# Transposing q and k of a token in one full-height product, in three parts instead of two

## The chip, the core and the metric

The kernel runs on one core of a Trainium2 chip. A core has five engines that each work through their own list of instructions in order and wait for each other by semaphores: TensorE (PE in the profile; PEld is its loading of the stationary operand), VectorE (DVE), ScalarE (ACT), GpSimd (POOL) and SyncE (SP). Here POOL issues nearly all loads and SP issues small transfers and the stores. TensorE reads operands from the on-chip memory SBUF and writes to PSUM; VectorE and ScalarE copy from there. The metric is the device time of one execution, in microseconds (us): a median of 444.62 over 7 runs (444.22 to 445.11).

## The reference

Two layers in a row: causal attention with a decay bias, and a spectral mixing layer on its output.

```python
# q, k, v: (8, 8, 576, 64), s: (8, 8, 576)
scores = scale * np.matmul(q, k.transpose(0, 1, 3, 2))
cum = np.cumsum(np.maximum(s, 0.0), axis=-1)
bias = -(cum[:, :, :, None] - cum[:, :, None, :])
scores = np.where(causal, -1000000000.0, scores + np.minimum(bias, 0.0))
attn = np.exp(scores - max);  attn = attn / (sum + 1e-09)
x = np.matmul(attn, v)                       # heads put side by side: (8, 576, 512)

X = np.fft.rfft(x, axis=1)                   # the lowest 64 modes are mixed:
Yr = Xr @ w_r[m] - Xi @ w_i[m]               # w_r, w_i: (64, 512, 512), one matrix for each mode
Yi = Xr @ w_i[m] + Xi @ w_r[m]
u = x + np.fft.irfft(Y, n=576, axis=1)
out = u + np.maximum(u @ w_ch, 0.0)
```

The mode weights are 2 x 64 x 512 x 512 float32 numbers, 134 MB, and are read once. They are most of what the kernel reads from device memory.

## The kernel before

**Steps.** The 64 pairs of batch and head are worked off two heads at a time: step n of 32 has batch b = n % 8 and the heads 2g and 2g + 1 of group g = n // 8 (N = 32, NG = 4). The main loop (L564 to L590) writes for each step, in this order: POOL's loads for later steps (`load`, L568), a row of decay sums by SP (`cum_rows`, L569), scores of the first head (`scores(n, 0)`), the weighted sum of v for the second head of the step before (`av(n - 1, 1)`), mode products if due (`mode_products`), the first half of the transposes for the next step (`transposes(n + 1, 0)`), scores of the second head, the second half of the transposes, the forward Fourier product of the step before (`fft(n - 1)`), `av(n, 0)`. The order is written out by hand, and each engine keeps to it: no scheduler moves anything.

**Transposes.** q and k come as one tile of 128 partitions: 64 for q, 64 for k, each (head, group of 18 tokens) on a partition, 18 tokens of 64 numbers in a row. One load brings two steps (`loads_qk`, two buffers). `scores` needs them with the 64 numbers of a token on partitions, in `qt` and `kt` (two buffers each). So each token slot r of 18 is transposed by TensorE into PSUM (`tr_ps`, pool `tr_psum`, one buffer), and copied from there. The 18 slots go in two halves of nine. In a half, every slot takes two products of 64 rows and 64 columns: q's rows give partitions 0 to 63 of `tr_ps`, k's rows partitions 64 to 127. Then q's part is copied to `qt` by VectorE, and k's to `kt` by VectorE in the first half and by ScalarE in the second (L341 to L347). As `tr_ps` has one buffer, a half waits until both copies of the half before are done. The copy of k by ScalarE starts after the copy of q from the same tile.

**What stands around them.** `scores` (L366) makes two tiles of 128 x 896 for a head, one for even and one for odd keys, and ScalarE takes the exponential of each in two pieces (L390); in the second head `scores4` adds a small one (L361). Mode products (`modes(g, c)`, L455) multiply the transformed x of group g by the weights of chunk c: 8 modes, four weight tiles, 16 products; 8 chunks make a group. Chunks of group g run during the steps of later groups at fixed places (`mode_steps`); those of the last group run after the loop (L833 to L868). In steps 26 to 31 the loop also prepares parts of the last product with `w_ch` (`first_transposed`, L529, and `first_product`, L540): transposes of x into `xt_ps`, a copy by VectorE (L538), a product (L546).

**Loads.** POOL holds one list of loads in program order, q, k and v mixed with weights (`load`, L230). A weight tile lies in a ring of 11 or 6 buffers (`wpool`, `wpool2`), so its load waits until the products of the tile that lay there are done; a load of q and k waits for the transposes of the steps that used its buffer.

**The tail.** After the loop come the products with `w_ch` that are left (`x_transposed`, L629, with products L635, and `x_times_wch`, L648), the last group's chunks 0 to 7, the inverse transform (`gather` L688, `add_y`, `add_last`) and the sums and stores.

Of the kernel before, what the change touches and what calls it, by code (L numbers as in the profile page):

```python
# [11 lines left out]
BF16 = mybir.dt.bfloat16  # L12
# [6 lines left out]
def kernel(  # L19
# [11 lines left out]
    nc = tc.nc  # L31
    B, H, S, D = q.shape
    NM = moe_w_r.shape[0]
    DM = H * D
    P = 128
# [15 lines left out]
    NF = NT - 1  # L51
    RP = P // 4
    R = S // RP
    RH = R // 2
    W = 2 * P
    NWN = S // W
    NK = 2 * NWN
# [1 line left out]
    HP = P // 2  # L59
# [81 lines left out]
    ident16 = ap_.tile([P, P], BF16, name="ident16")  # L141
# [4 lines left out]
    loaded = {}  # L146

    def loads_qk(n):

        if n >= N:  # L150
            return []
        g, b = divmod(n, B)
        hs = slice(2 * g, 2 * g + 2)
        t = loaded[n] = loaded[n + 1] = qkpool.tile([P, 2, R * D], BF16, name="qk2", tag="qk2")
        return [
            (
                t[HP * i : HP * i + HP, x0:x1],
                src[b + x0 : b + x1, hs].rearrange("b h (p r) d -> (h p) b (r d)", r=R),
            )
            for x0, x1 in ([(0, 2)] if n else [(0, 1), (1, 2)])  # L160
            for i, src in enumerate((q, k))
        ]

    def loads_v(n):

        if n >= N:
            return []
        g, b = divmod(n, B)
        return [
            (  # L170
                v2[n % NV][:, : 2 * NWN * W].rearrange("p (w h c) -> p w h c", w=NWN, h=2)[:, :, h, P:],
                v[b, 2 * g + h, : NF * P, :].rearrange("(w p r) d -> p w (r d)", p=P, r=2),
            )
            for h in range(2)
        ]
# [27 lines left out]
    def ring_of(k):  # L203
        if k < NE:
            return None
        return int(k < LW2 and (k - NE) % (WA + WB) >= WA)
# [23 lines left out]
    def load(*lists):  # L230

        todo = [((i + 0.5) / len(l), x) for l in lists for i, x in enumerate(l)]
        for _, (dst, src) in sorted(todo, key=lambda t: t[0]):
            nc.gpsimd.dma_start(out=dst, in_=src)  # L234
# [10 lines left out]
    for n in range(N):  # L245
# [3 lines left out]
        while nt < min(w, len(wq)):  # L249
            i = ring_of(nt)  # L250
# [36 lines left out]
    with tc.tile_pool(name="cum_psum", bufs=1, space=PSUM) as cpsum:  # L287
# [5 lines left out]
            out=cum, data0=spos, data1=zer, initial=0.0, op0=ALU.add, op1=ALU.add  # L293
# [16 lines left out]
        for x in range(2):  # L310
            rows = slice(NL * x, NL * x + NL)
            nc.vector.tensor_copy(
                out=cumt4[rows, :], in_=cumt_sb[rows, NK, x::2]
# [10 lines left out]
    def cum_rows(n):  # L324
        if n >= N:
            return
        g, b = divmod(n, B)
        p0 = b * H + 2 * g
        for h in range(2):
            nc.sync.dma_start(out=qt[n % NQ][D : D + 1, h, :], in_=ncum_sb[p0 + h : p0 + h + 1, :])  # L330

    def transposes(n, half):
        if n >= N:
            return
        src = loaded[n][:, n % 2, :].rearrange("p (r d) -> p r d", d=D)[:, half * RH : half * RH + RH]
        ps = trpool.tile([P, RH, 2 * RP], BF16, name="tr_ps", tag="tr")
        for r in range(RH):
            for i in range(2):
                rows = slice(HP * i, HP * i + HP)
                nc.tensor.transpose(ps[rows, r, :], src[rows, r, :], ident16[rows, rows])  # L340
        for i, dst in enumerate((qt, kt)):  # L341
            copy = (nc.vector.tensor_copy, nc.scalar.copy)[half * i]
            to = dst[n % NQ][:D].rearrange("d h (p r) -> d h p r", r=R)
            copy(  # L344
                out=to[:, :, :, half * RH : half * RH + RH],
                in_=ps[HP * i : HP * i + HP].rearrange("d r (h p) -> d h p r", h=2),
            )  # L347

    def scores4(n, ps):
# [45 lines left out]
    def first_token(b, T):  # L395

        if b % 2 == 0:
            return T * P
        return T * P + NL if T < NF else 0

    def av(n, h):
        if n < 0:
            return
        g, b = divmod(n, B)
        pt = p_sb[(2 * n + h) % NP_]
        ps = avpool.tile([P, NT, VW], FP32, name="av_ps", tag="av")
        todo = []
        for I in range(NT):
            t0 = first_token(b, I)
            for x in range(2 * min((t0 + P - 1) // W + 1, NWN)):  # L410
                w, r = divmod(x, 2)
                o = poff[x] + t0 - w * W
                todo.append((I, r, pt[:, o : o + P], v2[n % NV][:, bass.ds((2 * w + h) * W + P - 1 + NCH * r, NCH)]))
        rows = slice(NL * h, NL * h + NL)
        todo.append((NT - 1 - b % 2, 1, p4[n % 2][rows, :], v4[g % 2][rows, b, :NCH]))

        for i, (I, r, lhsT, rhs) in enumerate(todo):
            nc.tensor.matmul(  # L418
                ps[:, I, r : r + NCH], lhsT, rhs, start=(i == 0), stop=(i == len(todo) - 1),
                skip_group_check=True,  # L420
            )
        den = rpool.tile([P, NT], FP32, name="den", tag="den")
        nc.vector.tensor_reduce(  # L423
            out=den, in_=ps[:, :, 0 : VW : NCH], axis=mybir.AxisListType.X, op=ALU.add
        )
        rcp = rpool.tile([P, NT], FP32, name="rcp", tag="rcp")
        nc.vector.reciprocal(out=rcp, in_=den)
        nc.vector.tensor_tensor(  # L428
            out=x_all[:, g, b, :, D * h : D * h + D],
            in0=ps[:, :, 1 : NCH],  # L430
            in1=rcp.unsqueeze(2).to_broadcast([P, NT, D]),
            op=ALU.mult,
        )

    def fft(n):
        if n < 0:
            return
        g, b = divmod(n, B)
        ps = auxpool.tile([P, 2, 3 * HM], FP32, name="ft_ps", tag="aux")
        for T in range(NT):  # L440
            nT = tails[T]
            for q_ in range(2):
                nc.tensor.matmul(  # L443
                    ps[HP * q_ : HP * q_ + HP].rearrange("p h f -> p (h f)"),
                    x_all[:nT, g, b, T, q_::2], Ff_sb[:nT, T, :],
                    start=(T == 0), stop=(T == NT - 1),
                    tile_position=(0, HP * q_), skip_group_check=True,
                )
        for h in range(2):
            for q_ in range(2):  # L450
                a = ps[HP * q_ : HP * q_ + HP, h, : 2 * HM].rearrange("p (r m) -> p r m", r=2)
                a = bass.AP(tensor=a.tensor, offset=a.offset, ap=[a.ap[0], [HM, 2]] + list(a.ap[1:]))
                nc.vector.tensor_copy(out=xs[g % 2][HP * h : HP * h + HP, q_, :, h, :, b, :], in_=a)  # L453
# [98 lines left out]
    def mode_products(n):  # L552
        for c in mode_steps.get(n, []):
            modes(c // NCK, c % NCK)

    with tc.tile_pool(name="sc_psum", bufs=2, space=PSUM) as scpool, \
            tc.tile_pool(name="tr_psum", bufs=1, space=PSUM) as trpool, \
            tc.tile_pool(name="av_psum", bufs=1, space=PSUM) as avpool:
        cum_rows(0)
        transposes(0, 0)  # L560
        transposes(0, 1)
        load(loads_qk(2) + loads_v(2))
        pad_p()
        for n in range(N):  # L564
            if n in (0, 2):
                nc.vector.memset(xs_flat[n // 2].bitcast(FP32), 0.0)
            tails_due = loads_tails(n // B + 1)[n % B - 3 : n % B - 2] if 2 < n % B < 5 else []
            load((loads_qk(n + LA) if n % 2 else []) + loads_v(n + LA) + tails_due, loads_w(on_chip[n]))  # L568
            cum_rows(n + 1)  # L569
            scores(n, 0)  # L570
            av(n - 1, 1)
            if n % B:
                mode_products(n)
            transposes(n + 1, 0)
            scores(n, 1)
            i = first_pairs[n - N + len(first_pairs)] if n >= N - len(first_pairs) else None
            if i is not None:
                first_transposed(i, 0)
            transposes(n + 1, 1)
            fft(n - 1)  # L580
            av(n, 0)
            if i is not None:
                first_product(i, 0)
                first_transposed(i, 1)
            if n % B == 0:
                mode_products(n)
            if i is not None:
                first_product(i, 1)
            if n == N // 2:
                nc.gpsimd.dma_start(out=wch_sb, in_=moe_w_ch.rearrange("(dt p) e -> p dt e", p=P))  # L590
        av(N - 1, 1)
        fft(N - 1)
# [278 lines left out]
    for x in range(2):  # L871
        dts = slice(x * DT // 2, (x + 1) * DT // 2)
        ps = auxpool.tile([P, DT // 2, P], FP16, name="yt_ps", tag="aux")
# [49 lines left out]
    for step in (  # L923
# [8 lines left out]
        i = int(step[1:].rstrip("ab"))  # L932
# [34 lines left out]
```

The softmax here doesn't subtract the row's maximum and nothing guards it: scores larger than these inputs give would overflow.

## Time and profile before

The profiled execution took 445.11 us, the slowest of the seven; its span, from the first to the last instruction, is 443.0 us. It has 10783 instructions.

| engine | busy, us | share of the span |
|---|---|---|
| TensorE, products | 341.2 | 77% |
| TensorE, loading | 207.2 | 47% |
| VectorE | 253.1 | 57% |
| ScalarE | 226.4 | 51% |
| GpSimd | 246.1 | 56% |

| group of instructions | count | busy, us | mean, ns |
|---|---|---|---|
| transposes of q and k, TensorE L340 | 1152 | 35.3 | 206 |
| copy to qt, VectorE L344 | 64 | 47.8 | 748 |
| copy to kt, VectorE L344 | 32 | 24.4 | 763 |
| copy to kt, ScalarE L344 | 32 | 22.9 | 714 |
| exponentials, ScalarE L390 | 256 | 141.8 | 636 |
| mode products, TensorE L463 | 480 | 43.7 | 420 |

How to read it: products overlap on TensorE, so that the mean of one is longer than its share of the busy time. The first transposes start at 10.9 us and the last at 318.9; the first mode product starts at 80.3, and the last group's chunks run from 336.5 to 409.2. Slices are 40 equal parts of the span, 11.1 us each. The row PEclk gives the clock that TensorE was granted, in tenths of the full one. A line of the timeline has start, duration, engine, source line, operation, output and inputs, how many were merged, and in brackets the idle time of the engine just before and what ended it. A line of a group has count, then busy time and mean, then idle time before and what ended it.

### The profile page before, as it was taken

The page shows a single profiled execution, that of the slowest core. Times are in us where ns is not written, and L with a number is a line of the kernel's source. Part 1 is how long each engine was busy: PE and PEld are TensorE (multiplying, and loading weights), DVE is VectorE, ACT ScalarE, POOL GpSimd, SP SyncE. Part 2 cuts the span into 40 slices and gives each one's busy share as a digit, 9 for nine tenths or more (in the row PEclk, how much of TensorE's full clock was granted, in tenths as well). Part 3 has the DMA queues.
Part 4 walks back from the last instruction along what each step waited for, and adds up shares of the span by engine and source line. Part 5 has one row for each costly group of instructions (what it writes and reads, how often), then busy time and mean ns, then how long its engine had stood idle before and what let it go on. Part 6 is the DMA issues. An engine that isn't in the chain of part 4 may idle for free.

```text
span 443.0 us, 10783 instructions
## 1 busy us (share of the span) xinstructions
PE 341.2 (77%) x4364; PEld 207.2 (47%) x4411; DVE 253.1 (57%) x574; ACT 226.4 (51%) x421; POOL 246.1 (56%) x385
## 2 busy tenths in 40 slices
PE   1787888997685996694946828888887997759994
PEld 0465665565353653362624415555554445423441
DVE  7677775676554664462634605767655454432696
ACT  1477885476544743472634504765650544220794
POOL 7766566555565656465656546465644444430495
PEclk9999998999978897887786958999997999977998
DMA  9999999999999999999999999999999999997398
GB/s 180 202 206 206 204 207 205 206 207 207 208 200 207 205 209 204 208 207 208 204 206 206 209 207 191 209 206 205 197 209 210 210 209 210 210 217 144 145 388 344
DMA packets 72768, 93.25 MB, mean 210 GB/s; under 512 B 29760, under 2 KB 31296, under 8 KB 72720
## 3 DMA queue, kind: packets, MB, share of 16 engines
q0 software_dynamic: 63408, 81.29, 104.6%
q1 hardware_dynamic: 9312, 11.29, 7.6%
q8 instruction: 34, 0.56, 0.5%
q14 instruction: 14, 0.11, 0.1%
HBM read 163.51 MB, written 9.44 MB: 390 GB/s over the span
## 4 chain that ended last, share of the span: by engine, by line
DMA 69%; PE 15%; DVE 6%; POOL 5%; issue 4%; ACT 1%; POOLq 0%; DVEq 0%
DMA w_sb<-in_moe_w_i_dram 37%; DMA w_sb<-in_moe_w_r_dram 16%; DMA qk<-in_k_dram 8%; DMA qk<-in_q_dram 4%; PE yp L463 3%; DMA x_all<-in_moe_w_r_dram 2%; PE sc_ps L382 2%; DMA y_acc<-in_moe_w_r_dram 2%; POOL w_sb L234 1%; PE sc_ps L376 1%; PE tr_ps L340 1%; DVE xs L453 1%; DVE qt L344 1%; POOL v L234 1%; PE av_ps L418 1%
## 5 line engine op out<-in xcount | busy, mean ns | idle before, releaser
L390 ACT ACTIVATE p_sb<-sc_ps,cumt_sb 128x576 f16<-128x576 f32 (+1 forms) x256 | 141.8, 636 | 33.2 <-PE sc_ps L382 32.8
L234 POOL DMA_DIRECT2D w_sb<-in_moe_w_r_dram x120 | 71.2, 595 | 59.6 <-DMA w_sb<-in_moe_w_r_dram 18.9
L234 POOL DMA_DIRECT2D w_sb<-in_moe_w_i_dram x120 | 71.0, 593 | 54.3 <-DMA w_sb<-in_moe_w_i_dram 17.7
L344 DVE COPY qt<-tr_ps 64x576 bf16<-64x576 bf16 x64 | 47.8, 748 | 59.5 <-PE tr_ps L340 59.4
L234 POOL DMA_DIRECT2D v<-in_v_dram x72 | 52.0, 722 | 39.0 <-DMA w_sb<-in_moe_w_r_dram 9.5
L382 PE MATMUL sc_ps<-qt,kt 128*128 128x320 bf16 (+2 forms) x337 | 66.7, 303 | 6.6 <-ACT kt L344 1.9
L340 PE MATMUL tr_ps<-ident,qk 64*64 64x64 bf16 x1152 | 35.3, 206 | 41.3 <-DMA qk<-in_k_dram 18.2
L463 PE MATMUL yp<-w_sb,xs 128*32 128x512 bf16 (+1 forms) x480 | 43.7, 420 | 21.4 <-DMA w_sb<-in_moe_w_i_dram 14.2
L361 ACT ACTIVATE p<-sc_ps,cumt 128x64 f16<-128x64 f32 x32 | 10.1, 314 | 89.5 <-PE sc_ps L357 89.5
L376 PE MATMUL sc_ps<-negm,ident 128*128 128x256 bf16 x256 | 54.1, 296 | 0.0
L340 PEld LDWEIGHTS <-qk 64*64 64x64 bf16 x1152 | 26.9, 119 | 57.6 <-DMA qk<-in_k_dram 19.1
L382 PEld LDWEIGHTS <-kt 128*128 128x128 bf16 x384 | 39.1, 106 | 30.8 <-ACT kt L344 8.1
L418 PE MATMUL av_ps<-v,p_sb 128*128 128x65 f16 x1024 | 43.0, 195 | 1.9 <-DVE x_all L428 0.9
L418 PEld LDWEIGHTS <-p_sb 128*128 128x128 f16 x1024 | 36.4, 98 | 9.4 <-DVE x_all L428 4.9
L453 DVE CAST xs<-ft_ps 64x128 bf16<-64x128 f32 x128 | 36.7, 286 | 3.1 <-PE ft_ps L443 1.7
L463 PEld LDWEIGHTS <-xs 128*32 128x32 bf16 (+1 forms) x512 | 19.2, 144 | 39.5 <-DMA w_sb<-in_moe_w_i_dram 15.2
L423 DVE TENSOR_REDUCE den<-av_ps 128x5 f32<-128x10 f32 x64 | 10.8, 169 | 39.7 <-PE av_ps L418 38.7
L428 DVE TENSOR_TENSOR x_all<-av_ps,rcp 128x320 f16<-128x320 f32 x64 | 31.5, 492 | 2.2
L344 ACT COPY kt<-tr_ps 64x576 bf16<-64x576 bf16 x32 | 22.9, 714 | 15.5 <-DVE qt L344 14.8
L648 PE MATMUL z_ps<-wch_sb,xs 128*128 128x512 f16 x96 | 26.1, 420 | 0.2 <-DVE xs L639 0.2
L443 PE MATMUL ft_ps<-Ff_sb,x_all 128*64 128x192 f16 (+1 forms) x320 | 24.5, 267 | 1.0 <-DVE x_all L428 1.0
L344 DVE COPY kt<-tr_ps 64x576 bf16<-64x576 bf16 x32 | 24.4, 763 | 0.4
(113 smaller groups left out, 423.6 us busy)
## 6 DMA issues: line engine op xcount, KB each, us to landing
w_sb<-in_moe_w_r_dram POOLq DMA_DIRECT2D x120, 256.0 KB, 8.4
w_sb<-in_moe_w_i_dram POOLq DMA_DIRECT2D x117, 256.0 KB, 9.0
out_dram<-r_w SPq DMA_DIRECT2D x16, 512.0 KB, 2.8
v<-in_v_dram POOLq DMA_DIRECT2D x72, 64.0 KB, 7.4
qk<-in_q_dram POOLq DMA_DIRECT2D x15, 288.0 KB, 8.0
qk<-in_k_dram POOLq DMA_DIRECT2D x15, 288.0 KB, 9.2
x_all<-in_moe_w_i_dram POOLq DMA_DIRECT2D x6, 256.0 KB, 7.7
y_acc<-in_moe_w_r_dram POOLq DMA_DIRECT2D x4, 256.0 KB, 7.2
```

The lines of the kernel that those rows point to most:

```text
L234: nc.gpsimd.dma_start(out=dst, in_=src)
L340: nc.tensor.transpose(ps[rows, r, :], src[rows, r, :], ident16[rows, rows])
L344: copy(out=to[:, :, :, half * RH : half * RH + RH], in_=ps[HP * i : HP * i + HP].rearrange("d r (h p) -> d h p r", h=2),)
L376: nc.tensor.matmul(ps[:, bass.ds(w * S, W)], ident16, negm[:, bass.ts(r, W)], start=True, stop=False, skip_group_check=True,)
L382: nc.tensor.matmul(ps[:, c0 : c0 + i1 - i0], keys[:, w, r, :], qh[:, i0:i1], start=False, stop=True, skip_group_check=True,)
L390: nc.scalar.activation(out=pt[:, poff[x] : poff[x] + S - w * W], in_=ps[:, w * S : (w + 1) * S - w * W], func=ACTF.Exp, bias=cumt_sb[:, x, ...
L418: nc.tensor.matmul(ps[:, I, r : r + NCH], lhsT, rhs, start=(i == 0), stop=(i == len(todo) - 1), skip_group_check=True,)
L428: nc.vector.tensor_tensor(out=x_all[:, g, b, :, D * h : D * h + D], in0=ps[:, :, 1 : NCH], in1=rcp.unsqueeze(2).to_broadcast([P, NT, D]), ...
L443: nc.tensor.matmul(ps[HP * q_ : HP * q_ + HP].rearrange("p h f -> p (h f)"), x_all[:nT, g, b, T, q_::2], Ff_sb[:nT, T, :], start=(T == 0), ...
L453: nc.vector.tensor_copy(out=xs[g % 2][HP * h : HP * h + HP, q_, :, h, :, b, :], in_=a)
L463: nc.tensor.matmul(ps[32 * cg : 32 * cg + 32, :], cols[k0:, q_, 1 - ri, :, c * MC // 2 + cg], wt[(g, c, ri, cg // 2)][k0:, 2 * (cg % 2) + ...
L648: nc.tensor.matmul(zs[i, x], xts[i][:, x, dt, :], wch_sb[:, dt, :], start=(dt == 0), stop=(last and dt == DT - 1), skip_group_check=True,)
```

## The change

`transposes` goes from two halves to three thirds of six slots (`RH = R // 3`). A slot now takes one product over all 128 partitions, whose output has the 64 numbers on partitions 0 to 63 and q's and k's 64 columns side by side; `tr_ps` has 64 partitions of 6 x 128. The copies read both from the same 64 partitions: q by VectorE in all thirds, k by VectorE in the first and by ScalarE in the second and third. In the loop the third part stands between `fft(n - 1)` and `av(n, 0)`.

```diff
-    RH = R // 2
+    RH = R // 3
...
-    def transposes(n, half):
+    def transposes(n, third):
...
-        src = loaded[n][:, n % 2, :].rearrange("p (r d) -> p r d", d=D)[:, half * RH : half * RH + RH]
-        ps = trpool.tile([P, RH, 2 * RP], BF16, name="tr_ps", tag="tr")
+        part = slice(third * RH, third * RH + RH)
+        src = loaded[n][:, n % 2, :].rearrange("p (r d) -> p r d", d=D)[:, part]
+        ps = trpool.tile([HP, RH, P], BF16, name="tr_ps", tag="tr")
         for r in range(RH):
-            for i in range(2):
-                rows = slice(HP * i, HP * i + HP)
-                nc.tensor.transpose(ps[rows, r, :], src[rows, r, :], ident16[rows, rows])
+            nc.tensor.transpose(ps[:, r, :], src[:, r, :], ident16)
         for i, dst in enumerate((qt, kt)):
-            copy = (nc.vector.tensor_copy, nc.scalar.copy)[half * i]
+            copy = nc.scalar.copy if i and third else nc.vector.tensor_copy
             to = dst[n % NQ][:D].rearrange("d h (p r) -> d h p r", r=R)
             copy(
-                out=to[:, :, :, half * RH : half * RH + RH],
-                in_=ps[HP * i : HP * i + HP].rearrange("d r (h p) -> d h p r", h=2),
+                out=to[:, :, :, part],
+                in_=ps[:, :, HP * i : HP * i + HP].rearrange("d r (h p) -> d h p r", h=2),
             )
...
-        transposes(0, 0)
-        transposes(0, 1)
+        for third in range(3):
+            transposes(0, third)
...
             transposes(n + 1, 1)
             fft(n - 1)
+            transposes(n + 1, 2)
             av(n, 0)
```

## The prediction

> **What bounds the kernel now.** I read the page first (slices, chain), then the waits by engine, then the timeline of one late step of the attention loop, then that of the tail.
>
> ```profile
> PEclk9999998999978897887786958999997999977998
> DMA  9999999999999999999999999999999999997398
> GB/s 180 202 206 206 204 207 205 206 207 207 208 200 207 205 209 204 208 207 208 204 206 206 209 207 191 209 206 205 197 209 210 210 209 210 210 217 144 145 388 344
> DMA 69%; PE 15%; DVE 6%; POOL 5%; issue 4%; ACT 1%; POOLq 0%; DVEq 0%
> ```
>
> For 36 of 40 slices the DMA engines are full at 200 to 210 GB/s: POOL's one list of loads, nearly all mode weights, sets the pace until about 407 us. TensorE is beside it, but not far beside it: it sits idle for q and k 32.2 us in all (18.2 and 14.0 in the waits), every such wait lying before 237 us; from 270 to 400 it waits only 5.1 us for weights. So a TensorE delay before 237 is free as long as POOL's list stays fed; a delay after that has a few us to vanish in.
>
> One step late in the loop, TensorE then ScalarE:
>
> ```profile
> 295.37 0.47 PE L340 MATMUL tr_ps<-ident,qk 64*64 64x64 bf16 x18
> 295.77 0.39 PE L376 MATMUL sc_ps<-negm,ident 128*128 128x256 bf16 x2
> ...
> 297.70 0.47 PE L340 MATMUL tr_ps<-ident,qk 64*64 64x64 bf16 x18
> 298.10 0.72 PE L443 MATMUL ft_ps<-Ff_sb,x_all 128*64 128x192 f16 x10
> 298.76 0.67 PE L418 MATMUL av_ps<-v,p_sb 128*128 128x65 f16 x16
> ```
>
> ```profile
> 297.01 2.20 ACT L390 ACTIVATE p_sb<-sc_ps,cumt_sb 128x576 f16<-128x576 f32 x4
> 299.24 0.72 ACT L344 COPY kt<-tr_ps 64x576 bf16<-64x576 bf16 x1
> ```
>
> A half's 18 products hold TensorE for 0.40 us (295.37 to 295.77). ScalarE's exponentials of the second head run until 299.21, and only then comes its copy of k: 0.5 us after av has begun on TensorE. Nobody waits for that copy here.
>
> The tail:
>
> ```profile
> 353.13 0.88 PE L463 MATMUL yp<-w_sb,xs 128*32 128x512 bf16 x10
> 355.36 0.65 PE L463 MATMUL yp<-w_sb,xs 128*32 128x512 bf16 x6 [1.36 <-DMA w_sb<-in_moe_w_i_dram]
> 355.95 0.62 PE L635 MATMUL xt_ps<-ident16h,x_all 128*128 128x128 f16 x8
> 356.40 0.81 PE L648 MATMUL z_ps<-wch_sb,xs 128*128 128x512 f16 x3
> ...
> 393.38 1.51 PE L463 MATMUL yp<-w_sb,xs 128*32 128x512 bf16 x10 [1.88 <-DVE yv L709]
> 397.40 1.07 PE L463 MATMUL yp<-w_sb,xs 128*32 128x512 bf16 x6 [2.51 <-DMA w_sb<-in_moe_w_i_dram]
> ...
> 408.60 0.65 PE L463 MATMUL yp<-w_sb,xs 128*32 128x512 bf16 x4
> ```
>
> ```profile
> 397.64 0.59 POOL L234 DMA_DIRECT2D w_sb<-in_moe_w_i_dram  x1 [1.24 <-DMA w_sb<-in_moe_w_i_dram]
> ```
>
> Two weight waits are the slack of the tail. The last weight transfer is issued at 397.64 and lands 10.0 us later by the DMA view, at 407.6; its products start at 408.60. No speed of TensorE can bring the end forward by more than 1.0 us while the loads stand.
>
> **The change, part by part.**
>
> ```profile
> L390 ACT ACTIVATE p_sb<-sc_ps,cumt_sb 128x576 f16<-128x576 f32 x128 | 94.9, 741 | 33.2 <-PE sc_ps L382 32.8
> L390 ACT ACTIVATE p_sb<-sc_ps,cumt_sb 128x320 f16<-128x320 f32 x128 | 68.0, 531 | 0.0
> L344 ACT COPY kt<-tr_ps 64x576 bf16<-64x576 bf16 x32 | 22.9, 714 | 15.5 <-DVE qt L344 14.8
> ```
>
> *Products.* 36 per step become 18, each with 128 moving columns. The nearest row with 128 rows and 128 moving columns is x_transposed, L635: 8 products in 0.45 us (355.95 to 356.40), 0.056 each. A third then costs 6 x 0.056 = 0.34 us and a step 1.02, against 2 x 0.40 = 0.80: +0.22 us. From below: an old pair, side by side, takes 0.40/9 = 0.044 us for 64 columns, and one product with 128 columns will not take less, so no gain: 18 x 0.044 = 0.80, the old price. From above: the gather's products (L699, weights 128*64, 128 moving) take 0.62 us for eight, two column halves at a time, so up to 0.155 for one, +2.0 us a step. I take 0.056, the row with one full-height product at a time.
>
> [...]
>
> *Copies.* Six of 384 elements for four of 576. ScalarE pays (741 - 531)/256 = 0.82 ns an element, so 714 - 192 x 0.82 = 557 ns; VectorE, by 748 ns for 576 and 286 for 128 (L453), 1.03 ns, so 748 - 198 = 550 (763 becomes 565). VectorE 4 x 0.55 = 2.2 us against 2.26; ScalarE 1.11 against 0.71. Neither engine is the bound (57% and 51% busy).
>
> *The wait.* tr_ps has one buffer, so each part waits until both copies of the part before have left it. Part 1 waits for VectorE copies only, now 1.1 us instead of 1.5: in the early steps its wait of 0.46 us goes, in the late ones there was none to gain but once 0.23. Part 2 is new: it stands between fft and av(n,0), and needs ScalarE's copy of part 1, which queues behind the exponentials. In the step above: exponentials end at 299.15 (the first third frees 0.06 us), copy until 299.73, part 2 from 299.78 to 300.12, and av starts there, not at 298.76: 1.36 us late. Queued behind the wait on TensorE are av(n,0), the kept product and the whole next step. POOL and SP get no new instruction.
>
> *Late steps, 26 to 30* (no transposes in 31). Lateness of av: 1.40, 1.18, 1.36, 1.36, 1.40. In four of them TensorE later waits about 1.0 us for VectorE's xt cast, of which 0.2 shrinks away; I get 1.18 + 1.00 + 1.36 + 1.15 + 1.15 = 5.8 us at the first mode product of the last group (336.50 becomes 342.3). With both bounds of a product: 5 to 11 us.
>
> *Early steps.* From 52.60 to 59.23 a step is 6.6 us. By the same chain, part 2 runs from 57.03 to 57.37; the copies of q (VectorE) and k (ScalarE waits for it, same tile) end at 58.65, and the next scores start at 58.7 for 57.24: a step becomes 8.1 us. Eight steps leave TensorE some 10 us late where it used to wait for q and k. The waits of 32 us swallow this by about step 22, so I cost it at nothing. Its cover is the queue: a load lands 7 to 9 us after its issue, while the stores at the end, with little before them, land in 2.0 to 2.8, so POOL may stand still for some 5 us. Buffers freed late stop it. A q and k buffer is now free only after part 2: for the load at 39.31 the old part 1 ended at 35.7, the new part 2 would at 40.8, a stop of 1.5 us. The weight load at 90.90 needs the products of the first group's chunk 2 (until 84.4, then about 95), a stop of 4 us. If a stop is longer than the cover, every later transfer is late by the excess.
>
> *Tail.* The last group's chunk 2 (353.13) comes 5.8 us late, and all its weights are there: its 16 products take 1.02 us, not 2.82, so 1.80 us are swallowed; 0.2 more at 385.43. Chunk 6 starts at 393.38 + 3.8 = 397.2. Its weights land at 397.40, so it does not wait, but at the clock of that place (0.65 in 390 to 400) it needs 1.51 + 1.07 us: it ends at 399.8 instead of 398.47. **Sum: +1.3 us**, and all behind it (PE, then ScalarE and POOL) shifts by that. 445.11 us (span 443.0 and 2.1 around it) becomes 446.4. That execution was the slowest of seven; against their median of 444.62 the forecast is 445.9.
>
> **The rivals.**
>
> *Clock stays up in the tail (not slower).* The granted clock is half at 338 to 345 and 393 to 403, each after a stretch with gaps (7.0 us with 4.1 busy at 331 to 338). If lateness fills the gap of 394.9 to 397.4, the clock stays full there: chunk 6 ends at 398.3, and the 4.8 us of work until 403.2 take half. Then the last weights bind, 1.0 us before today: 443.6. It decides when the clock is full there. Against it: a third more stalls make more gaps. [...]
>
> *The lateness is lost earlier (not slower).* If the first spell does not come, 3 us of the 5.8 vanish, and the second weight wait eats the rest: 444.6. It decides when TensorE is less than 2.5 us late at chunk 6.
>
> *POOL runs dry.* If a product costs 0.1 us or more, early steps exceed 8.5 us, the stop at 91 us grows past 6 us, and late steps lose 8: I put the end 3 to 5 us later, 448 to 450. For it: buffers there are freed with only 6.5 us to spare. Against it: 8.4 us median landing.
>
> *The wait is not there.* If ScalarE's copy came before the exponentials, only +0.22 x 5 = 1.1 us would remain, inside the slack: 444.6. Its place in the program's order is behind them, so I give it little and count it with the lateness lost earlier.
>
> **How the numbers follow.** A change within 0.2%, 0.9 us, can't be told from none here. The forecast (445.5 to 447.5, its own range) 0.40; the clock stays up 0.25, of which 0.09 lies just beyond 0.9 us faster, at the bound that the last weights set; the lateness lost earlier 0.20; POOL runs dry 0.12; something slower that I don't see 0.03. Slower 0.40 + 0.12 + 0.03 = 0.55, same 0.36, faster 0.09. The range for 8 in 10 takes in the clock case down to its bound and the lower part of the dry queue: 443.5 to 448.8; left out is the rest of that queue and the unseen.
>
> **What will show it.** Right: part 2 of each step preceded by a wait for ScalarE's kt copy of about 1 us; av(n,0) 1.2 to 1.4 us later after part 1; the wait for kt on VectorE at part 1 gone; the waits for q and k down by 20 us or more; PE at chunk 2 of the last group without its 1.36 us wait; GB/s unchanged until 400. Wrong: GB/s below 195 in a slice near 90 or 110 us; a product well off 0.056 us; the clock full from 393 to 403.

## The result and the profile after

The changed kernel takes 447.33 us (median of 15, from 444.86 to 448.96) against 444.68 (median of 36, 443.86 to 445.85) for the kernel before: the ratio is 1.0056, with a 95% interval of 1.0043 to 1.0068. It is slower, by 2.65 us at the medians. The forecast was 445.9 with a range of 443.5 to 448.8; the time lies inside it, in the forecast case's own range (445.5 to 447.5), but the loss is twice the 1.3 us of the sum.

The times of the changed kernel spread over 4 us (5 with the second series below), those of before over 2 to 3. So I show two profiled executions of it: a *first* one of 445.79 us, near the fast end, and a *second* one of 447.49 us, at the median. Slices and chain, the first execution:

```profile
PEclk9988999998899899997797978999999999988998
GB/s 177 202 206 204 187 202 205 206 205 205 207 202 208 204 208 201 209 207 208 203 206 206 208 207 206 208 206 206 208 210 209 210 211 209 209 216 130 181 385 310
DMA 38%; PE 34%; ACT 15%; DVE 5%; issue 4%; POOL 2%; SPq 0%; POOLq 0%; DVEq 0%
```

The second execution, the same rows:

```profile
PEclk9999988999999999897986959998999799988998
GB/s 181 202 197 205 204 207 204 207 207 206 207 203 206 206 208 204 208 207 208 203 208 206 208 206 205 207 207 203 203 210 210 210 210 209 210 217 83 178 384 310
PE 42%; DMA 27%; ACT 15%; DVE 9%; issue 3%; POOL 3%; SPq 0%; POOLq 0%; DVEq 0%; ACTq 0%
```

The loads run at the old rate in both (one slice of 187 at 44 to 55 us aside). In the kernel before, transfers were 69% of the chain that ended last; here that falls to 38%, and in the median execution to 27%, with TensorE at 42%. In the median execution TensorE has become the bound for the last part of the program.

The waits of TensorE (second column of numbers: how often, then the longest), first execution:

```profile
PE tr_ps L339 <- ACT kt L343: 35.4, 32, 1.7
PE tr_ps L339 <- DMA qk<-in_k_dram: 12.5, 3, 6.7
PE z_ps L545 <- DVE xt L537: 5.8, 6, 1.8
```

The new wait is there in every step, 35.4 us in all. The waits for q and k have shrunk from 32.2 us to 12.5 (15.9 in the second execution): the early part of the new wait was taken out of them. One late step, TensorE and then ScalarE:

```profile
310.67 0.52 PE L339 MATMUL tr_ps<-ident,qk 128*64 128x128 bf16 x6
311.13 0.39 PE L375 MATMUL sc_ps<-negm,ident 128*128 128x256 bf16 x2
...
312.94 0.41 PE L339 MATMUL tr_ps<-ident,qk 128*64 128x128 bf16 x4
...
314.96 0.49 PE L339 MATMUL tr_ps<-ident,qk 128*64 128x128 bf16 x6 [0.97 <-ACT kt L343]
315.39 0.67 PE L417 MATMUL av_ps<-v,p_sb 128*128 128x65 f16 x16
```

```profile
312.36 2.20 ACT L389 ACTIVATE p_sb<-sc_ps,cumt_sb 128x576 f16<-128x576 f32 x4
314.43 0.48 ACT L343 COPY kt<-tr_ps 64x384 bf16<-64x384 bf16 x1
```

Part 2 stands still for 0.97 us until ScalarE, done with the exponentials, has copied k of part 1. From the first part to av it is 4.72 us (310.67 to 315.39); in the kernel before it was 3.39 (295.37 to 298.76). Where the lateness goes, by the starts of the last group's chunks:

| | before | changed, first | changed, second |
|---|---|---|---|
| chunk 0 starts | 336.50 | 343.02 | 343.69 |
| chunk 1 starts | 347.43 | 351.69 | 354.17 |
| chunk 2 starts | 353.13 | 357.40 | 359.87 |
| chunk 6 starts / ends | 393.38 / 398.47 | 395.21 / 397.87 | 397.69 / 399.20 |
| chunk 7 starts | 404.17 | 404.03 | 405.71 |
| last weight load issued | 397.64 | 397.03 | 395.99 |
| last store issued | 439.48 | 439.35 | 441.04 |
| span | 443.0 | 444.0 | 445.7 |

Both are some 7 us late at chunk 0. Some 5.5 us of that were made in the late steps from 276 us on. The first was 1.0 us late before them; the second was on time there, and lost 1.7 us in a spell of half clock (0.51 granted from 306 to 309 us) behind one of the waits. The first then loses 2.3 us of its lateness by chunk 1, the second 0.5. The reason is the clock there. Busy times of the engines and, third number from the right, the granted clock, first execution:

```profile
337.00:344.00 7.00, 4.09 (x47) 2.18 (x44) 4.02 (x14) 1.17 (x2) 3.54 (x6) 1.00 1.12 210
344.00:351.00 7.00, 5.92 (x50) 3.39 (x50) 4.44 (x8) 1.72 (x4) 3.10 (x6) 1.00 1.13 210
```

Second execution:

```profile
337.00:344.00 7.00, 4.08 (x46) 2.29 (x44) 4.13 (x14) 1.50 (x3) 2.93 (x5) 0.97 1.12 209
344.00:351.00 7.00, 6.53 (x37) 3.02 (x34) 3.93 (x7) 0.00 (x0) 3.54 (x6) 0.54 1.13 210
```

The same 4.1 us of work in seven went before, and the clock fell in one and stayed up in the other. The half clock costs 1.8 us (chunk 0 to 1 takes 10.48 us for 8.67). In the same two stretches it fell, too, with part 1's k by VectorE (0.78 and 0.73) and with part 2 behind av in the late steps (0.73 and 0.79), two kernels of the next section without extra products. It fell in the kernel before as well (0.52 from 338 to 345 us), where the later waits for weights (1.36 and 2.51 us) swallowed it. The second execution then has no slack left at chunk 6:

```profile
397.69 1.51 PE L462 MATMUL yp<-w_sb,xs 128*32 128x512 bf16 x16 [1.88 <-DVE yv L709]
400.47 0.61 PE L672 MATMUL yt_ps<-ident16h,y_sb 128*128 128x128 f16 x4 [0.30 <-DVE y_sb L486]
405.71 0.68 PE L462 MATMUL yp<-w_sb,xs 128*32 128x512 bf16 x8
```

No wait for weights is left (2.51 us before), and chunk 7 comes 1.54 us late, which reaches the last store unchanged. The first execution still waits 0.70 us for weights and is level with before at chunk 7. So the lateness is made in the late steps, and whether it reaches the end hangs on spells of the clock. The last weight load was issued earlier than before in both: the load queue has no part in it.

One piece is not of this making. From the last store's issue to the end of the span it is 3.55 us in the execution before and 4.6 to 4.7 in these two, while a trickle of some 25 GB/s is still moving. That is 1.1 of the second execution's 2.7 us of longer span (2.4 us in its time, 447.49 for 445.11); the section on the hardware comes back to it.

### The profile page after: what moved, and what is told of

The parts are those of the page before. It is cut to its first block, busy times and chain, and to the rows that moved or that the text cites. A ratio compares the mean times of both kernels' runs of the same rounds, so it can differ in the third digit from the quotient of the medians.

```text
span 444.0 us, 9723 instructions
## 1 busy us (share of the span) xinstructions
PE 345.8 (78%) x3797; PEld 218.4 (49%) x3835; DVE 249.6 (56%) x606; ACT 230.5 (52%) x453; POOL 246.2 (55%) x385
## 4 chain that ended last, share of the span: by engine, by line
DMA 38%; PE 34%; ACT 15%; DVE 5%; issue 4%; POOL 2%; SPq 0%; POOLq 0%; DVEq 0%
DMA w_sb<-in_moe_w_i_dram 27%; ACT p_sb L389 9%; DMA w_sb<-in_moe_w_r_dram 7%; PE sc_ps L381 7%; PE tr_ps L339 5%; PE av_ps L417 5%; PE yp L462 4%; PE sc_ps L375 4%; ACT kt L343 3%; DMA qk<-in_k_dram 2%; DVE qt L343 2%; ACT p L360 1%; PE z_ps L545 1%; DMA xs<-c_negm 1%; POOL w_sb L234 1%
## 5 line engine op out<-in xcount | busy, mean ns | idle before, releaser
L339 PE MATMUL tr_ps<-ident,qk 128*64 128x128 bf16 x576 | 52.9, 232 | 49.1 <-ACT kt L343 35.4
L343 DVE COPY qt<-tr_ps 64x384 bf16<-64x384 bf16 x96 | 52.5, 546 | 54.9 <-PE tr_ps L339 54.7
L381 PE MATMUL sc_ps<-qt,kt 128*128 128x320 bf16 (+2 forms) x346 | 68.4, 304 | 5.9 <-ACT kt L343 1.5
L339 PEld LDWEIGHTS <-qk 128*64 128x64 bf16 x576 | 39.9, 116 | 63.8 <-issue 43.3
L343 ACT COPY kt<-tr_ps 64x384 bf16<-64x384 bf16 x64 | 30.6, 479 | 50.6 <-DVE qt L343 50.4
L462 PE MATMUL yp<-w_sb,xs 128*32 128x512 bf16 (+1 forms) x480 | 39.8, 410 | 12.0 <-DMA w_sb<-in_moe_w_i_dram 6.2
L417 PE MATMUL av_ps<-v,p_sb 128*128 128x65 f16 x1024 | 44.9, 199 | 0.0
L417 PEld LDWEIGHTS <-p_sb 128*128 128x128 f16 x1024 | 40.1, 101 | 4.8
L442 PE MATMUL ft_ps<-Ff_sb,x_all 128*64 128x192 f16 (+1 forms) x320 | 27.8, 257 | 1.0 <-DVE x_all L427 1.0
L375 PEld LDWEIGHTS <-ident 128*128 128x128 bf16 x256 | 18.3, 100 | 10.3 <-issue 2.3
```

Of the source, the lines that this page charges most:

```text
L339: nc.tensor.transpose(ps[:, r, :], src[:, r, :], ident16)
L343: copy(out=to[:, :, :, part], in_=ps[:, :, HP * i : HP * i + HP].rearrange("d r (h p) -> d h p r", h=2),)
L375: nc.tensor.matmul(ps[:, bass.ds(w * S, W)], ident16, negm[:, bass.ts(r, W)], start=True, stop=False, skip_group_check=True,)
L381: nc.tensor.matmul(ps[:, c0 : c0 + i1 - i0], keys[:, w, r, :], qh[:, i0:i1], start=False, stop=True, skip_group_check=True,)
L417: nc.tensor.matmul(ps[:, I, r : r + NCH], lhsT, rhs, start=(i == 0), stop=(i == len(todo) - 1), skip_group_check=True,)
L442: nc.tensor.matmul(ps[HP * q_ : HP * q_ + HP].rearrange("p h f -> p (h f)"), x_all[:nT, g, b, T, q_::2], Ff_sb[:nT, T, :], start=(T == 0), ...
```

## The experiments

Medians in us; each kernel was timed beside the kernel before on the same chip. The ratio weighs all times and not the medians alone, so it can differ from the quotient of the two columns: with three parts and 64-row products, four of twelve times lie at 447.6 to 448.5 us and lift it.

| kernel | time | before | ratio, 95% interval | chunk 0 |
|---|---|---|---|---|
| changed, again | 447.59 | 444.43 | 1.0053, 1.0032 to 1.0074 | 343.69 |
| new parts in late steps only | 445.91 | 444.43 | 1.0031, 1.0011 to 1.0050 | 342.50 |
| new parts in early steps only | 444.83 | 444.43 | 1.0004, 0.9992 to 1.0017 | 336.76 |
| part 1's k by VectorE | 445.29 | 444.43 | 1.0018, 1.0003 to 1.0033 | 340.87 |
| three parts, 64-row products | 445.38 | 444.54 | 1.0035, 1.0013 to 1.0056 | 342.05 |
| part 2 behind av, all steps | 448.73 | 444.54 | 1.0100, 1.0081 to 1.0119 | 346.22 |
| part 2 behind av, late steps | 445.22 | 444.41 | 1.0016, 1.0004 to 1.0027 | 339.04 |
| changed + products in step 31 | 443.52 | 444.54 | 0.9984, 0.9967 to 1.0001 | 342.12 |
| the same again | 443.84 | 444.41 | 0.9991, 0.9972 to 1.0010 | 342.55 |
| before + products in step 31 | 444.90 | 444.41 | 1.0015, 0.9999 to 1.0030 | 336.31 |
| before + products at chunk 6 | 445.02 | 444.54 | 1.0008, 0.9995 to 1.0022 | 336.65 |
| part 2 late + products in step 31 | 444.16 | 444.41 | 1.0001, 0.9983 to 1.0019 | 339.44 |

### Where: late steps, early steps, or loads

The changed kernel once more:

> The changed kernel once more, for a second profiled execution and more times: the fifteen known times lie between 444.9 and 449.0 us (median 447.3), and the one execution that was profiled is at their lower end (445.8). The theory of the late steps expects the first product of the last group again at about 343 us for 336.5 before, whatever the total. If the total is high, the theory expects the excess behind 336 us (TensorE at half clock in a spell that the first profile did not have, or the weights of chunks 6 and 7 later). The theory of the load queue expects the excess as a slice with less than 200 GB/s ahead of 336 us and the last weight load issued later than 397.6 us by as much.

Measured 447.59 us; its profile is the second execution above. The excess lies behind 336 us, and the last load is early (395.99): the late steps, not the queue. Over the 28 executions of this kernel that have their clock on record, the mean granted clock and the time go against each other (correlation -0.73): the two fastest, 443.72 and 444.15, had 0.951 and 0.952, the ten above 448 us 0.927 to 0.940.

```diff
     def transposes(n, third):
         if n >= N:
             return
+        if n < 25:
+            if third == 2:
+                return
+            return two_parts(n, third)
```

Here two_parts is the function of the kernel before, with its halves and its order. This is the edit for late only; for early only the condition is `n >= 25`.

> Tokens of steps up to 24 transposed as before (two halves, 64-row products), those of step 25 and later in three full-height parts. Late-steps theory: the whole loss comes back, since TensorE is as late at the last group (342 to 343 us at its first product) as in the changed kernel: 446 to 447.5 us, ratio to before 1.003 to 1.006. Load-queue theory (early steps hold buffers longer): nothing is lost, 444.7 +- 0.5 us, ratio 0.999 to 1.001.

> The other way round: tokens of steps up to 24 in three full-height parts, later ones as before. Late-steps theory: the early lateness is swallowed by the waits for q and k, and the time is that of before, 444.7 +- 0.5 us, ratio 0.999 to 1.001. Load-queue theory: the loss of 2.6 us is here, 446 to 448 us, ratio 1.003 to 1.007, with the slice at 44 to 55 us below 195 GB/s and the last weight load issued later than 397.6.

Early only costs nothing that can be measured (1.0004, with chunk 0 at 336.76), though its TensorE waits 27.4 us for ScalarE's copies. Late only has chunk 0 at 342.50 and loses time, 1.0031; its twelve times run from 443.5 to 449.2, so that it can't be said whether it has the whole loss or part of it. So the cause sits in the late steps; what the early ones lose is swallowed.

### What in a late step: the wait or the products

```diff
-            copy = nc.scalar.copy if i and third else nc.vector.tensor_copy
+            copy = nc.scalar.copy if i and third == 2 else nc.vector.tensor_copy
```

> The changed kernel with the k copy of part 1 by VectorE, so that part 2 no longer stands behind ScalarE's exponentials. VectorE's two copies (0.55 us each) end about 1.2 us after part 1, and fft covers 0.66 of it: the wait ahead of part 2 falls from 0.97 to about 0.5 us in the late steps. Late-steps theory: 5 x 0.45 = 2.2 us less lateness, the first product of the last group at 340.5 to 341.5 us, and about half of the loss gone: 445.5 to 446 us, ratio 1.001 to 1.004. Load-queue theory: a step of the early stretch shrinks from 7.65 to about 7.2 us, the stop at 40 to 44 us by one to two us, and the time to about 446. If the wait is not the cause at all, 447.3 us.

```profile
312.96 0.52 PE L339 MATMUL tr_ps<-ident,qk 128*64 128x128 bf16 x6 [0.72 <-DVE kt L343]
```

The wait falls to 0.72 us, less far than the 0.5 expected: VectorE starts its copies (at 311.90 us) only after an xt cast of 0.69 us that begins at 311.30. A late step shrinks by 0.2 us (11.31 to 11.09), chunk 0 moves to 340.87 and the ratio from 1.0056 to 1.0018, as the theory had it.

```diff
-        ps = trpool.tile([HP, RH, P], BF16, name="tr_ps", tag="tr")
+        ps = trpool.tile([P, RH, 2 * RP], BF16, name="tr_ps", tag="tr")
         for r in range(RH):
-            nc.tensor.transpose(ps[:, r, :], src[:, r, :], ident16)
+            for i in range(2):
+                rows = slice(HP * i, HP * i + HP)
+                nc.tensor.transpose(ps[rows, r, :], src[rows, r, :], ident16[rows, rows])
...
-                in_=ps[:, :, HP * i : HP * i + HP].rearrange("d r (h p) -> d h p r", h=2),
+                in_=ps[HP * i : HP * i + HP].rearrange("d r (h p) -> d h p r", h=2),
```

> Three parts, but each slot with two products of 64 rows, as before (twelve in a part). What is left of the change is the cut into thirds and its wait. Theory: a part costs 0.27 us for 0.45, and ScalarE's copy of part 1 comes as late as ever behind the exponentials, which start 0.18 us earlier; a late step costs about 0.75 us over before, for 1.1 with the full-height product; the first product of the last group at 340.3 to 341.3 us, 445.2 to 446.2 us, ratio 1.001 to 1.004. Rival: the wait alone is the cause and the product is free: 447.4 +- 0.5 us. Other rival: the product alone is the cause: 444.5 +- 0.4 us.

The time fits, the mechanism expected behind it does not: a late step takes 11.20 us, only 0.11 less than with the full-height product, and chunk 0 comes at 342.05. So of the 1.1 us that a late step grew, the product makes about 0.1 and the cut into three with its wait about 1.0. The first third is 0.15 us shorter here, but part 2 stands at the same 4.29 us after it, because ScalarE's copy now starts only when the last exponential has ended. VectorE shows the same with two copies in a row. Three parts with 64-row products, VectorE:

```profile
310.68 0.54 DVE L345 COPY qt<-tr_ps 64x384 bf16<-64x384 bf16 x1
311.23 0.56 DVE L345 COPY kt<-tr_ps 64x384 bf16<-64x384 bf16 x1
```

The changed kernel:

```profile
311.43 0.54 DVE L343 COPY qt<-tr_ps 64x384 bf16<-64x384 bf16 x1
311.89 0.54 DVE L343 COPY kt<-tr_ps 64x384 bf16<-64x384 bf16 x1
```

In the changed kernel q and k are read from the same partitions and the second copy starts 0.46 us after the first, before that has ended; with k on partitions 64 to 127 it starts 0.55 us after it. ScalarE's copy behaves alike: it starts 0.13 us before the last exponential ends (314.43 for 314.56) there, and 0.02 us after it here.

```diff
             fft(n - 1)
+            av(n, 0)
             transposes(n + 1, 2)
-            av(n, 0)
```

> The changed kernel with part 2 behind av(n, 0) instead of ahead of it. Theory: ScalarE's copy of part 1 ends while av runs (0.72 us), so the wait of 0.97 us in the late steps falls to 0.2 us or less, and only the price of the products is left (a third takes 0.45 us for an old half's 0.40): some 0.5 us a step for 1.1, the first product of the last group at 338.5 to 340 us, and 444.5 to 445.3 us, ratio 1.000 to 1.002. Rival: the wait moves to the next scores, which need part 2's copies; where these come as late as av did, the loss stays: 446.5 to 447.5 us.

This expectation fell: 448.73 us, worse than the change. The late steps did what was expected (the wait is down to 0.2 us, a step takes 10.57), but the early steps run 8.0 us or more, since the wait moved to the next scores, and what the third rival of the prediction describes came about: POOL ran dry. Transfer rates by slice, and POOL:

```profile
GB/s 180 202 199 206 204 207 204 203 150 190 207 203 206 205 208 204 209 206 208 203 206 208 206 207 207 208 206 206 208 209 209 210 209 210 209 217 115 204 373 288
```

```profile
97.98 0.59 POOL L234 DMA_DIRECT2D w_sb<-in_moe_w_r_dram  x1 [7.64 <-PE yp L462]
```

POOL stands 7.64 us for products of the first group, the ninth slice falls to 150 GB/s, and the last load goes out at 399.6 instead of 397.6 us. In the changed kernel the stop at this place is 0.98 us and costs nothing. Moved in steps 24 to 31 alone:

```diff
+            if n < N - 8:
+                transposes(n + 1, 2)
             av(n, 0)
+            if n >= N - 8:
+                transposes(n + 1, 2)
```

> The changed kernel with part 2 behind av(n, 0) only in steps 24 to 31; before that ahead of it, as in the changed kernel. Theory: moved in all steps it cost 4.3 us, because the early steps then run 8.0 us instead of 7.65 and one weight load (at 98 us) stood still for 7.6 us, longer than the transfers under way could cover; the late steps themselves gained (10.55 us against 11.3, before 10.2). Moved in the late steps alone, the load queue stays fed and TensorE reaches the last group about 2 to 3 us late instead of 6.5: 444.4 to 445.4 us, ratio 1.000 to 1.002. Rival: the lateness behind av is what costs, wherever it is: 446.5 us or more.

```profile
312.45 0.49 PE L339 MATMUL tr_ps<-ident,qk 128*64 128x128 bf16 x6 [0.23 <-ACT kt L343]
```

445.22 us, chunk 0 at 339.04 (2.5 us late), loads at the full rate: most of the loss is gone, as expected. The wait of part 2 in the late steps is the main cause of the lateness, and early lateness cost time here only where it stopped POOL longer than the transfers under way covered.

### The clock

```diff
+    def warm(pool, tag, k):
+        t = pool.tile([P, DM], FP32, name="warm", tag=tag)
+        for _ in range(k):
+            nc.tensor.matmul(t, ident16h, wch_sb[:, 0, :], start=True, stop=True)
...
+            if n == N - 1:
+                warm(trpool, "tr", 4)
...
         av(N - 1, 1)
+        warm(trpool, "tr", 4)
         fft(N - 1)
...
+    warm(upool, "u", 4)
     for c in range(NCK - 2):
```

> The changed kernel with three times four extra products (128 x 128 by 512, whose result nobody reads) in step 31 and behind the loop, at the three places where TensorE waits about 1 us each for VectorE (338 to 344 us). Theory: in most executions the clock falls to half there, from about 343.6 to 350 us, and TensorE has by then no slack left, so the spell's 1.8 us reach the end; in the rest it stays up, and the time is near that of before. The extra products keep the array busy, the spell goes, and all executions move to the lower group: median 444.5 to 446.0 us, chunk 1 of the last group at about 352 us for 354.2. Rival: the spread has another cause (loads, stores), and the median stays at 447.4 +- 0.5 us, or rises by the 2.6 us of the extra products if these delay TensorE.

> The changed kernel with the extra products once more, for a closer interval: 443.5 +- 0.6 us, ratio to before 0.997 to 0.999, if its first eight times (442.7 to 446.2) were no chance; 444.5 or more if they were.

```profile
337.00:344.00 7.00, 6.88 (x59) 2.95 (x56) 3.44 (x11) 0.80 (x2) 3.28 (x6) 1.00 1.12 209
344.00:351.00 7.00, 5.92 (x51) 3.37 (x55) 4.37 (x7) 2.34 (x5) 3.21 (x6) 1.00 1.14 211
```

The changed kernel with twelve idle products (nobody reads their result) falls to 443.52 and 443.84 us, some 3.8 us below the change alone; the waits of 1 us are filled, the clock stays up, and chunk 0 starts no later (342.12, 342.55). It is 0.6 to 1.0 us below the kernel before as well, but both intervals take in 1, so it is not shown to be faster. The loss thus needs both parts, the lateness and the spell. Not all slow times come from spells, though: one execution of this kernel took 447.45 us at a mean granted clock of 0.951. In the kernel before, where TensorE is not late:

> The kernel before with the same twelve extra products in step 31 and behind the loop that took the changed kernel to 443.5 us. Theory: in before TensorE is early, and what a full clock at 338 to 345 us gives back is waited away at the two weight waits behind it (355 and 397 us): 444.5 +- 0.4 us, ratio 0.999 to 1.001. Rival: the extra products speed up whatever kernel they are in: 443.5 us, ratio 0.9975.

```profile
352.31 0.43 PE L463 MATMUL yp<-w_sb,xs 128*32 128x512 bf16 x2 [0.96 <-DMA w_sb<-in_moe_w_i_dram]
354.81 0.98 PE L463 MATMUL yp<-w_sb,xs 128*32 128x512 bf16 x6 [2.07 <-DMA w_sb<-in_moe_w_i_dram]
```

No gain, 444.90 us: chunk 2 starts at 350.69 instead of 353.13 and waits the difference away. The second spell, in the kernel before:

```diff
+    warm(upool, "u", 4)
     yb6 = modes(NG - 1, c)
...
+                if g == NG - 1 and c == NCK - 2 and (x, z) == (2, 2):
+                    warm(upool, "u", 8)
```

> The kernel before with twelve extra products of the same kind around chunk 6 of the last group: four in the wait for VectorE ahead of it, eight in the wait for its weights (394.9 to 397.4 us). Theory: the half clock of 393 to 403 us costs before 1.0 us at the end (the last weights land at 407.6 and their products start at 408.6); filled gaps keep the clock up, and the last weights become the bound: 443.6 us, ratio 0.9975 to 0.999. Rival: the weights of chunk 6 are already the bound, or the extra products delay chunk 6 as much as the clock gives back: 444.4 to 445.5 us, ratio 1.000 to 1.002.

```profile
397.23 0.66 PE L463 MATMUL yp<-w_sb,xs 128*32 128x512 bf16 x6 [1.05 <-DMA w_sb<-in_moe_w_i_dram]
401.97 0.67 PE L463 MATMUL yp<-w_sb,xs 128*32 128x512 bf16 x8
```

The clock stayed up (eight products with `w_ch` took 1.90 us from 399.28 on, where before they took 3.51 from 399.86 on), chunk 7 started 2.2 us earlier and ended 1.2 earlier, and the last store was issued at 438.27 instead of 439.48; yet the profiled execution ended later than before (5.36 us after that store), and the median did not fall. In this one execution the theory of the clock held up to the last store and failed behind it. Both repairs of the late steps together:

> Both repairs of the late steps together: part 2 behind av in steps 24 to 31, and the extra products of step 31. TensorE is 2 to 3 us late at the last group and keeps its clock there; the last weights (landing at 406 to 407.6 us) are then the bound, as in the kernel with the extra products alone: 443.3 to 444.3 us, ratio 0.997 to 0.9995. If lateness still counted with the clock up, it would beat the kernel with the extra products alone by up to 1 us.

444.16 us: no better than the extra products alone. With the extra products in, 2.9 or 6 us of lateness make no difference that can be measured: TensorE waits for the weights of chunk 6 again (2.09 us here, 0.65 and 0.58 with the extra products alone). The last weights, which the expectation names, held TensorE up in only one of these three profiled executions, by 0.57 us.

## Why the prediction was right, and where it was not

*The wait: right.* 0.97 us in the late steps for about 1; av comes 1.33 us later after the first part for 1.36; the late steps make some 5.5 us of lateness for 5.8, and with what else came in, the first product of the last group is at 343.0 and 343.7 for 342.3. Taking the wait down (part 1's k by VectorE, part 2 behind av late) takes the lateness down, to 4.4 and 2.5 us, and most of the loss with it (1.0018 and 1.0016; the two can't be told apart).

*Products: the price of one right, that of a part mis-sized.* Single records of the trace give a full-height product 0.056 us after the one before, as taken from L635. What the sum left out is a fixed price of each new part. The old pairs follow each other every 0.032 us, not 0.044: I divided a half's 0.40 us by nine, and 0.12 of it is that fixed price. In the first third, the first product is followed after 0.080 us (in the last one, behind its wait, after 0.055), and the next operation's first product comes 0.151 after the last one; its weight load starts only then. Three parts take 1.19 us a step (0.455, 0.307 and 0.428; ahead of fft, whose products have 64 columns too, there is no gap) for 0.80, where the sum had 1.02: +0.39, not +0.22. The 0.151 us lie between products of 64 and of 128 columns (starts at 310.977 and 311.128 us). Ahead of fft the kernel before has 0.123 us (297.980 to 298.103), there behind products of 64 rows and 64 columns. What the engine does in that time was not shown.

*Early steps: right in kind.* 7.65 us a step for 8.1; waits for q and k down by 19.7 us in the first execution and 16.3 in the second for "20 or more"; nothing that can be measured reaches the end (early only, 1.0004).

*POOL's cover: right in size, off in its places.* In the first execution the stop at 39 us was 4.8 us long for 1.5, with one slice at 187 GB/s, and the one at 91 us 1.0 for 4. Neither moved the last load. That 7.6 us is too long, and 4.8 not, agrees with the "some 5 us" that the prediction allowed.

*Tail: the swallowing right, the clock half right.* In the median execution chunk 2 lost its 1.36 us wait and chunk 6 its weight wait, as the terms said. Chunk 6 ends 0.73 us late there for 1.3, since its products took 1.51 us and not the 2.58 of the sum. But the half clock then lasts until 405.0 us for 403.2, TensorE waits 0.30 us more for VectorE, and chunk 7 is 1.54 us late. The sum ended at chunk 6, and there the step "all behind it shifts by that" failed: 0.73 became 1.54, near the 1.3 of the sum by two errors that cancel. The rest of the difference, about 1.1 us of span, lies behind the last store, where the sum had nothing. That the median still lies in the case's own range, by 0.2 us, is in part luck: the sum had half of the loss.

*The rivals.* "The lateness is lost earlier" is what the first execution shows: no spell at 344 us, TensorE 1.8 us late at chunk 6, and chunk 7 level with before. The missing spell gave back 2.3 us, where the rival had 3. 7 of the 28 executions took less than 446 us. "The clock stays up" did not come: in both profiled executions of the changed kernel the half clock is there between 397 and 405 us, in the second although no wait for weights is left. The extra products bring the 443.6 us of this rival by another road; they take away the spell at 344 us, and the later one is still there (0.69 granted from 393 to 404 us in the first of the two). "POOL runs dry" came with steps of 8.0 us and part 2 moved, where the prediction had put it beyond 8.5. I had the spells as separate cases with one time each; the spell at 344 us comes and goes between executions of one kernel.

## What to carry to other kernels

A copy that is needed to free a single buffer should not queue behind the longest work of its engine: ask of every added part which engine's queue its buffer waits in. Look for slack behind the change, stage by stage: the same lateness cost nothing ahead of the waits for q and k, and it counted where the weights were already there. Where a program has gaps ahead of its critical part, look at the clock behind them in more than one execution (here 1.00 in one and 0.54 in the other, after 4.1 us of work in 7); a spread of times that grows after a change can be a sign that such a stretch has come onto the path.

## What the runs showed of the hardware

- The clock after a gap differs between executions of one program: 4.09 and 4.08 us of work in the 7 us before, then 1.00 and 0.54. With the gaps filled (6.88 us of work in 7, the changed kernel with products in step 31) it was 1.00 in both stretches; in the kernel before with the same products, the 16 products of chunk 1 took 1.09 us at 344.99, as long as at 1.00 in the changed kernel (357.40). What decides it was not shown.
- Two copies on VectorE overlap in the changed kernel, which reads q and k from the same partitions of PSUM: in all 32 first parts the copy of k starts 0.07 to 0.08 us before that of q has ended. In the kernel before, with k on the other half of the partitions, it starts 0.01 us after it, in all 32 first halves. ScalarE's copy of k, where it follows an exponential, starts 0.13 to 0.14 us before that has ended in 29 of 31 cases in the changed kernel, and in no case before it has ended in the kernel before (0.02 to 0.04 us after it in 24 of 31). Against three parts with 64-row products, the changed kernel has 0.09 us of this back from copy to copy (0.46 for 0.55). That the partitions alone decide it was not shown: the layout of the tile differs, too.
- Between the issue of the last store and the end of the span lie 3.5 to 3.7, 4.5 to 4.9 or 5.4 to 5.6 us, depending on the execution. In the longer ones some 25 GB/s move on behind the rest, here in the last 10 us of the kernel before with products at chunk 6 (slices of 0.25 us):

```profile
GB/s 377 442 385 377 369 393 410 401 401 344 401 434 401 401 393 418 401 410 410 402 426 410 393 401 352 33 25 25 25 25 25 25 16 0 0 0 0 0 0 0
```

What decides the length of this tail was not tried and stays open. The 14 profiled executions do not tie it to the change: kernels with the new parts had 3.5 to 5.6 us, the kernel before and its two variants 3.55, 3.62 and 5.36. So it stays open whether the 1.1 us of the second execution belong to the 2.65 us between the medians, or whether lateness makes up more of them than this execution shows. Open, too, are the executions of the changed kernel at 448 to 449 us, none of which was profiled, and why the last weight load goes out earlier in most kernels with the full-height parts (395.6 to 397.0 us for 397.3 to 397.6 in the three profiled executions without the new parts).
